# Decoding the last weight matrix during the attention and parking it in DRAM as float32

## The chip, the core and the metric

The kernel runs on one core of one Trainium2 chip. A core has five engines that run side by side, each with its own queue of instructions, which it takes strictly in order: PE (TensorE, matrix products; its weight loads are listed apart as PEld), DVE (VectorE), ACT (ScalarE), POOL (GpSimd) and SP (SyncE, which here only issues DMAs). Engines wait for one another through semaphores. Matrix products are accumulated in PSUM (eight banks), everything else lies in SBUF or in DRAM. The metric is the device time of one execution in microseconds (us); lower is better.

## What is computed

Three stages, each fed by the one before:

```python
attn_out = _attn_ref(q, k, v, f)                # 4 batches, 8 heads, 576 positions, 64 per head
x = attn_out.transpose(0, 2, 1, 3).reshape(2304, 512)
h = (x @ w1) * (x @ w2)                         # 512 -> 1024
x = (h @ w3) @ w_out                            # 1024 -> 1024 -> 512
h = x @ w_in                                    # 512 -> 2048
P = a[0] + a[1]*h + a[2]*h**2 + a[3]*h**3
Q = 1 + abs(b[0])*abs(h) + abs(b[1])*h**2
out = (P / (Q + 1e-6)) @ w_out2                 # 2048 -> 512
```

The attention adds to the scores a decay from the running sum of log f, masks the future, takes a softmax, and multiplies by v. All weight matrices arrive as float64. The kernel reads a weight as a pair of 32-bit integers and builds a float32 from the bits. That is called decoding here. Products that need more than one pass run three matmuls on a value split in two parts (high and low, with names that end in h and l).

## The kernel before

The program is one hand-ordered stream; the order in which Python issues an instruction is the order in its engine's queue.

**The decoder** (class Decoder, lines 38 to 114) has a list of jobs, one for each piece of a weight matrix: 128 rows by 256 columns (512 for w1 and w2). A ring of d_r buffers takes the loads of int64 pairs, and a second ring, d_f, the float32 result. One call of `step` works on four pieces at once, one in each phase: for piece k two DVE instructions (lines 99 and 102) and one of ACT (line 105, in place in d_r); for piece k-1 the POOL add (line 95) that finishes the float32; for piece k-2 the ACT copy that rounds the high part (line 91); for piece k-3 the subtraction that gives the low part (line 88, DVE or POOL in turn). Then `prefetch` issues the next load on SP (line 67), which waits until the ring's buffer is free, that is, for the POOL add of that same step. A list of n pieces needs n + 3 steps.

**The attention** (lines 547 to 651) runs 32 heads of five columns each; t counts the columns, n is the head, c the column. In each, PE makes scores, transposes the probabilities of an earlier column and multiplies by v; DVE takes the maximum (line 324), splits (line 381), evacuates ps_v (lines 256 and 411); ACT takes the exponential; POOL normalises (line 350). From head 9 on, `fill` puts matmuls of stage one (`gen_ab`, x times w1 and w2) between them, at 123 credits a matmul. Each pair of products is finished by an ACT copy a_sb (line 475) and a DVE product c_sb (line 478), which is stored to c_dr on SP. These free the PSUM banks for the next pair. `side_step` advances the decoder of w1 and w2, in the columns of DEC_AT and in every even column from t = 46, until it is done; the rest of it is run in head 13 at column 0 (line 416).

**The drain** (lines 699 to 711) comes next: the last batch of `gen_ab`, alone on PE, with four banks; after each 1250 credits `flush(2)` issues the copies and products that are due and the decoder makes one step. This second decoder, dec_, has a ring of four and takes w3 (32 pieces), w_out (16) and w_in (32), and in the kernel before also w_out2, called wo2 below (32).

**The w3 stage** (lines 738 to 763) multiplies w3 by w_out, so that stage three needs one product only; it transposes w3 row by row on PE and makes four decoder steps per row.

**Stage three** (lines 797 to 820) makes z = c times that product in nine blocks of four outputs, 24 matmuls an output, with banks in rotation. The block of c is loaded to cl and split (line 429, DVE, after an ACT copy to ch) one block ahead; z goes through z_sb (three buffers) to z_dr. The decoder makes one step after an even output and two after an odd one. The last stage (lines 891 to 921) uses w_in and wo2.

Of the kernel before, what the change touches and what calls it, by code (L numbers as in the profile page):

```python
# [10 lines left out]
F32 = mybir.dt.float32  # L11
# [8 lines left out]
P = 128  # L20
# [13 lines left out]
def raw(ap):  # L34
    return ap.bitcast(F32)


class Decoder:
# [8 lines left out]

    def __init__(self, nc, pool, name, size, n_ring, n_f32, jobs, lo_on="v", ahead=None):  # L50
        self.nc, self.jobs, self.lo_on = nc, jobs, lo_on
        self.ring = [pool.tile([P, size, 2], I32, name=f"{name}_r{i}") for i in range(n_ring)]
        self.f32 = [pool.tile([P, size], F32, name=f"{name}_f{i}") for i in range(n_f32)]
        self.at = 0
        self.sent = 0
        self.more = False
        self.ahead = n_ring if ahead is None else ahead
        self.prefetch()
# [18 lines left out]
    def step(self):  # L77

        nc, k, n = self.nc, self.at, len(self.jobs)
        if k >= n + (0 if self.more else 3):  # L80
            return False
        if 0 <= k - 3 < n:
            _, _, hi, lo = self.jobs[k - 3]
            if hi is not None:
                on = self.lo_on[(k - 3) % len(self.lo_on)]
                eng = nc.vector if on == "v" else nc.gpsimd
                v = self.like(self.place(k - 3), hi)
                eng.tensor_tensor(out=lo, in0=v, in1=raw(hi), op=ALU.subtract)
        if 0 <= k - 2 < n and self.jobs[k - 2][2] is not None:
            hi = self.jobs[k - 2][2]  # L90
            nc.scalar.copy(hi, self.like(self.place(k - 2), hi))
        if 0 <= k - 1 < n:
            u = self.place(k - 1).bitcast(I32)
            r = self.ring[(k - 1) % len(self.ring)]
            nc.gpsimd.tensor_tensor(out=u, in0=u, in1=r[:, :, 0], op=ALU.add)  # L95
        if k < n:
            r = self.ring[k % len(self.ring)]
            u, high, low = self.place(k).bitcast(I32), r[:, :, 1], r[:, :, 0]
            nc.vector.tensor_scalar(  # L99
                u, high, 3, -0x40000000, op0=ALU.logical_shift_left, op1=ALU.bitwise_or  # L100
            )
            nc.vector.scalar_tensor_tensor(  # L102
                out=u, in0=high, scalar=0x3FFFFFFF, in1=u, op0=ALU.bitwise_or, op1=ALU.bitwise_and
            )
            nc.scalar.activation(low, low.bitcast(U32), AF.Copy, scale=2.0**-29)  # L105
        self.at += 1
        self.prefetch()
        return True
# [9 lines left out]
def kernel(  # L118
# [40 lines left out]
    def pool(name, side, **kw):  # L159
        return tc.tile_pool(name=name, bufs=1, side=side, reuse_waits="tile", **kw)  # L160

    dram = ctx.enter_context(tc.tile_pool(name="dram", bufs=1, space=DRAM))
    crow_dr = dram.tile([NH, 2, S], F32, name="crow_dr")
    c_dr = dram.tile([P, NF1, NT], F32, name="c_dr")
    z_dr = dram.tile([P, NKC, NT], F32, name="z_dr")

# [264 lines left out]
    def gen_w12():  # L431
# [18 lines left out]
        xh.append(x1p.tile([P, NKC, S], F32R, name="xh1"))  # L450
        xl.append(x1p.tile([P, NKC, S], F32R, name="xl1"))

    def gen_ab(b, more=()):
        banks = [*ps_f, *more]
        X, L = xh[b % 2], xl[b % 2]
        n = 0
        FG = PIECE2 // P
        for g, hf, fi in itertools.product(range(NF1 // FG), range(2), range(FG)):
            ts_ = slice(HB * hf, HB * (hf + 1))
            fi += FG * g  # L460
            fs = slice(P * fi, P * (fi + 1))
            w12["dec"].run(4 * g + 3)
            outs = [t[:, 0:HB] for t in banks[n % (len(banks) // 2) * 2 :][:2]]
            for wi, nm in enumerate(("w1", "w2")):
                wh, wl = w12[nm]
                flush(len(banks) // 2)
                for kc in range(NKC):
                    mm(outs[wi], wh[:, kc, fs], X[:, kc, ts_], kc == 0, False)
                    yield 123
                    mm(outs[wi], wh[:, kc, fs], L[:, kc, ts_], False, False)  # L470
                    yield 123
                    mm(outs[wi], wl[:, kc, fs], X[:, kc, ts_], False, kc == NKC - 1)
                    yield 123
                if wi == 0:
                    pend.append(lambda a=a_sb[n % 2], o=outs[0]: nc.scalar.copy(a, o))

            def finish(c=c_sb[n % 3], a=a_sb[n % 2], fi=fi, hf=hf, o=outs[1]):
                nc.vector.tensor_tensor(out=c, in0=o, in1=a, op=ALU.mult)
                nc.sync.dma_start(c_dr[:, fi, S * b + HB * hf : S * b + HB * (hf + 1)], c)

            pend.append(finish)
            n += 1
# [6 lines left out]
    def flush(keep=0):  # L489
        while len(pend) > keep:  # L490
            pend.pop(0)()
# [5 lines left out]
    def fill(ns):  # L497
        credit[0] += ns
        while credit[0] > 0 and fillers:
            cost = next(fillers[0], "end")  # L500
            if cost == "end":
                fillers.pop(0)
            elif cost is None:
                break
            else:
                credit[0] -= cost
        if not fillers:
            credit[0] = 0.0
# [38 lines left out]
    for t in range(NCH * (NH + 1) + 2):  # L547
# [35 lines left out]
        flush()  # L583
        if t == 10:
            w12["dec"].ahead = 4
        if t in DEC_AT or (t >= 46 and t % 2 == 0):
            side_step()
        if t == 0:
            first_q(1)
# [61 lines left out]
                load_pair(p + 1, vf[(p + 1) % 2] if 2 * (p + 1) < N32 else v_raw, v)  # L651
    fill(1.0e9)
    flush()
    late.close()
    att.close()
    fillers.append(gen_ab(B - 1, (ps_v[:, 0:512], ps_v[:, 512:1024])))
# [48 lines left out]
    credit[0] = 0.0  # L705
    fill(3000.0)
    while fillers:
        fill(1250.0)
        flush(2)
        dec_.step()  # L710
    flush()
# [54 lines left out]
    wl_ = ctx.enter_context(pool("wl", "right"))  # L766
    woh = wl_.tile([P, NF2, DM], F32R, name="wo2h")
    wol = wl_.tile([P, NF2, DM], F32R, name="wo2l")
    for j in range(NF2):
        w_jobs(w_out2, j, woh, wol)  # L770
    dec_.more = False
    dec_.prefetch()
    ps1.close()
    psp = ctx.enter_context(tc.tile_pool(name="psp2", bufs=1, space=PSUM, reuse_waits="tile"))
    bank = [psp.tile([P, 512], F32, name=f"bank{i}") for i in range(8)]
# [21 lines left out]
    for i in range(NBLK):  # L797
        if 0 < i < NBLK - 1:
            load_c(i + 1)
        for e in range(NKC):  # L800
            g = NKC * i + e
            po = bank[g % 8][:, 0:T1]
            es = slice(P * e, P * (e + 1))
            for fi in range(NF1):
                mm(po, w3oh[:, fi, es], ch[i % 2][:, fi], fi == 0, False)
                mm(po, w3oh[:, fi, es], cl[i % 2][:, fi], False, False)
                mm(po, w3ol[:, fi, es], ch[i % 2][:, fi], False, fi == NF1 - 1)
            if g > 1:
                z_store(g - 2)
            if g > 0:  # L810
                z_out(g - 1)
            for _ in range(1 + g % 2):
                dec_.step()
            if i + 1 < NBLK:
                for x in ((), (0,), (2, 4), (6,))[e]:
                    split_c(i + 1, x)
        if i == NBLK - 2:
            load_z(0)
            for e in range(NKC):
                split_z(0, e)  # L820
# [137 lines left out]
```

## Time and profile before

| | us |
|---|---|
| median of three runs | 1047.26 (1044.64 to 1049.3) |
| the profiled execution | 1044.14 |
| its span, first to last instruction | 1042.3 |
| busy in the span: PE, DVE, ACT, POOL | 988.6, 811.1, 677.5, 386.2 |

The profile is one execution taken by the hardware profiler, with times from the start of the span. Busy times are sums over a stretch. Matmuls are pipelined, so a PE that is busy all the time may still be slowed. A row of waits tells which instruction stood idle for which. The granted clock is 1.00 at 2.4 GHz and 0.50 at 1.2 GHz.

### The profile page before, as it was taken

Reading aid. Unit: us, or ns where it says so; the run is one execution under the profiler, and the core shown is the slowest. Engines: PE = TensorE matmul, PEld = TensorE weight load, DVE = VectorE, ACT = ScalarE, POOL = GpSimd, SP = SyncE. Lnnn points to the kernel's source line nnn. Section 1 sums busy time; section 2 is a strip of 40 time slices with the busy share of each in tenths; the row PEclk is TensorE's granted clock in tenths of the full one; section 3 lists DMA queues with packets and bytes.
Section 4 is the critical chain, followed back from the end, with each engine's and each line's share of the span. In section 5 each row is a group of like instructions: output and inputs, shape, how many; then the busy total and the mean of one; then the engine's idle time right before and its main releaser. Section 6 shows DMA issues by size and latency. Waiting matters only on the chain.

```text
span 1042.3 us, 18664 instructions
## 1 busy us (share of the span) xinstructions
PE 988.6 (95%) x6224; PEld 898.4 (86%) x6224; DVE 811.1 (78%) x1809; ACT 677.5 (65%) x1558; POOL 386.2 (37%) x482
## 2 busy tenths in 40 slices
PE   6887889999999999899989899999999999999998
PEld 4666779999999999888789898988999889988897
DVE  5788886666666664989988886888888888888886
ACT  5566566666666663535655556777777777777775
POOL 7444564333333332544555551222222222222221
PEclk9999899999999999999999999999999999999999
DMA  5868454454544312676567771010010000000000
GB/s 132 213 155 183 129 149 105 110 131 111 125 113 124 98 41 85 205 219 190 174 192 243 244 245 58 1 31 31 1 31 31 31 31 1 31 31 1 31 1 31
DMA packets 119569, 106.59 MB, mean 102 GB/s; under 512 B 64816, under 2 KB 89904, under 8 KB 119472
## 3 DMA queue, kind: packets, MB, share of 16 engines
q1 hardware_dynamic: 119472, 105.40, 36.1%
q8 instruction: 49, 0.80, 0.3%
q14 instruction: 48, 0.39, 0.1%
HBM read 66.41 MB, written 19.02 MB: 82 GB/s over the span
## 4 chain that ended last, share of the span: by engine, by line
PE 73%; DVE 13%; DMA 6%; issue 4%; POOL 2%; ACT 2%; SPq 0%; POOLq 0%; DVEq 0%; ACTq 0%
PE bank L157 42%; PE ps_f L157 14%; PE ps_s L157 5%; PE ps_v L157 4%; PE ps_x L355 4%; DVE d_f L99 3%; DMA d_r<-in_moe_w_dram 2%; DMA d_r<-in_moe_w_out_dram 2%; DVE d_f L102 2%; PE ps_w L157 2%; DVE cl L429 1%; PE ps_v L246 1%; DMA z_dr<-z_sb 1%; DVE w3r L102 1%; DVE pr L324 1%
## 5 line engine op out<-in xcount | busy, mean ns | idle before, releaser
L855 POOL TENSOR_TENSOR gl<-pp,gh 128x384 fp32r<-128x384 f32 x96 | 98.0, 1021 | 314.5 <-ACT gh L854 251.4
L350 POOL TENSOR_SCALAR pr<-pr,st 128x128 f32<-128x128 f32 (+4 forms) x160 | 93.5, 595 | 194.0 <-DVE st L345 75.6
L324 DVE CUSTOM_DVE_ANT_0 pr<-ps_s,mask 128x128 f32<-128x128 f32 (+4 forms) x160 | 83.1, 523 | 72.3 <-PE ps_s L157 69.8
L157 PE MATMUL bank<-ch,wih 128*128 128x384 f32 x384 | 129.1, 336 | 2.0 <-DVE pp L876 2.0
L157 PE MATMUL bank<-ch,wil 128*128 128x384 f32 x384 | 129.4, 337 | 0.0
L157 PE MATMUL bank<-cl,wih 128*128 128x384 f32 x384 | 128.6, 335 | 0.0
L335 ACT ACTIVATE pr<-pr,st 128x128 f32<-128x128 f32 (+4 forms) x160 | 97.1, 607 | 32.1 <-DVE st L324 31.7
L95 POOL TENSOR_TENSOR d_f<-d_f,d_r 128x256 int32<-128x256 int32 (+1 forms) x96 | 88.1, 918 | 78.9 <-DVE d_f L102 36.4
L157 PE MATMUL bank<-wo2h,gl 128*128 128x512 f32 x288 | 113.9, 395 | 0.0
L157 PE MATMUL bank<-wo2l,gh 128*128 128x512 f32 x288 | 113.5, 394 | 0.0
L157 PE MATMUL bank<-wo2h,gh 128*128 128x512 f32 x288 | 113.5, 394 | 0.0
L862 ACT ACTIVATE h<-bank 128x384 f32<-128x384 f32 x96 | 47.0, 489 | 87.1 <-PE bank L157 86.5
L157 PE MATMUL bank<-cl,w3oh 128*128 128x256 f32 x288 | 82.1, 285 | 8.4 <-DVE cl L429 8.4
L379 ACT CAST pth<-ps_x 128x256 fp32r<-128x256 f32 (+1 forms) x96 | 44.5, 464 | 67.8 <-PE ps_x L355 51.3
L157 PE MATMUL ps_s<-kh,qs 128*128 128x128 f32 (+2 forms) x192 | 75.9, 395 | 8.6 <-DVE st L324 5.4
L157 PE MATMUL bank<-ch,w3ol 128*128 128x256 f32 x288 | 81.4, 283 | 1.4 <-DVE w3ol L755 1.4
L355 PE MATMUL ps_x<-ident,pr 128*128 128x128 f32 (+1 forms) x480 | 75.0, 265 | 6.8 <-POOL pr L350 3.3
L157 PE MATMUL bank<-ch,w3oh 128*128 128x256 f32 x288 | 81.2, 282 | 0.0
L105 ACT ACTIVATE d_r<-d_r 128x256 int32<-128x256 uint32 (+1 forms) x128 | 60.0, 471 | 31.4 <-DMA d_r<-in_moe_w_dram 23.9
L157 PEld LDWEIGHTS bank<-ch,wih 128*128 128x128 f32 x384 | 72.0, 188 | 6.9 <-DVE pp L876 2.7
L879 DVE SCALAR_TENSOR_TENSOR qv<-qv,rr 128x384 f32<-128x384 f32 x96 | 53.5, 558 | 31.3 <-ACT rr L874 31.3
L869 DVE SCALAR_TENSOR_TENSOR qv<-h,pb_abs,qv 128x384 f32<-128x384 f32 x96 | 59.1, 616 | 23.5 <-ACT qv L863 23.5
(167 smaller groups left out, 3076.3 us busy)
## 6 DMA issues: line engine op xcount, KB each, us to landing
d_r<-in_moe_w_out_dram SPq DMA_DIRECT2D x48, 256.0 KB
c_dr<-c_sb SPq DMA_DIRECT2D x64, 144.0 KB
cl<-c_dr SPq DMA_DIRECT2D x36, 256.0 KB
d_r<-in_moe_w_dram SPq DMA_DIRECT2D x16, 512.0 KB
d_r<-in_moe_w_dram SPq DMA_DIRECT2D x32, 256.0 KB
d_r<-in_moe_w_in_dram SPq DMA_DIRECT2D x32, 256.0 KB
kh<-kh SPq DMA_DIRECT2D x45, 144.0 KB
z_dr<-z_sb SPq DMA_DIRECT2D x36, 128.0 KB
```

The source lines that it names most:

```text
L95: nc.gpsimd.tensor_tensor(out=u, in0=u, in1=r[:, :, 0], op=ALU.add)
L105: nc.scalar.activation(low, low.bitcast(U32), AF.Copy, scale=2.0**-29)
L157: nc.tensor.matmul(o, lhsT, rhs, start=start, stop=stop)
L324: nc.vector.tensor_tensor_reduce(out=pr[0:r, OFF[c] + a : OFF[c] + b], in0=ps_s[(t + part) % 2][0:r, 0 : b - a], in1=mask[0:r, 512 - Q0[c] ...
L335: nc.scalar.activation(x, x, AF.Exp, bias=st[0:r, 0, c : c + 1], scale=-1.0, accum_out=st[0:r, 1, c : c + 1],)
L350: nc.gpsimd.tensor_scalar(x, x, st[0:r, 1, c : c + 1], 1.0, op0=ALU.mult, op1=ALU.mult)
L355: nc.tensor.transpose(ps_x[x][:, r * j : r * (j + 1)], pr[0:r, o + P * j : o + P * (j + 1)], ident[0:r, 0:r],)
L379: nc.scalar.copy(hi, src)
L855: nc.gpsimd.tensor_tensor(out=at(gl, j), in0=at(pp, j), in1=raw(at(gh, j)), op=ALU.subtract)
L862: nc.scalar.activation(at(h2, i), h, AF.Square)
L869: nc.vector.scalar_tensor_tensor(out=at(qv, i), in0=at(h2, i), scalar=pb_abs[:, 1:2], in1=at(qv, i), op0=ALU.mult, op1=ALU.add,)
L879: nc.vector.scalar_tensor_tensor(out=at(qv, i), in0=at(qv, i), scalar=QC, in1=at(rr, i), op0=ALU.add, op1=ALU.mult)
```

## The change

The 32 pieces of wo2 leave the list of dec_. A generator, `gen_wo2`, decodes them during the attention: it starts in head 13 at column 0, with one step at once, and then steps in columns 1 and 3 of every head until it is through. It has rings of three. It keeps float32 only and stores each piece to a new DRAM tensor, wo2_dr, one step after its POOL add. In stage three the matrix comes back by eight loads of 512 KB, one every four outputs, and is split there by one ACT copy and one subtraction of 512 columns after every second output. Stage three makes one decoder step an output. The drain gives 1600 credits a step.

```diff
@@ Decoder.step
+        if 0 <= k - 2 < n and len(self.jobs[k - 2]) > 4:
+            nc.sync.dma_start(self.jobs[k - 2][4], self.place(k - 2))
@@ new generator
+    def gen_wo2():
+        jobs = []
+        for j in range(NF2):
+            for g in range(0, DM, PIECE2):
+                cs = slice(g, g + PIECE2)
+                jobs.append((w_out2[P * j : P * (j + 1), cs], None, None, None, wo2_dr[j, :, cs]))
+        with pool("d3", "right") as rp:
+            dec_ = Decoder(nc, rp, "d3", PIECE2, 3, 3, jobs)
+            while dec_.step():
+                yield
@@ attention loop
-        if t in DEC_AT or (t >= 46 and t % 2 == 0):
+        if t == 65:
+            while side:
+                side_step()
+            side.append(gen_wo2())
+            side_step()
+        if t in DEC_AT or (46 <= t < 65 and t % 2 == 0) or (t > 65 and c in (1, 3)):
             side_step()
@@ drain
-        fill(1250.0)
+        fill(1600.0)
@@ before stage three
-    for j in range(NF2):
-        w_jobs(w_out2, j, woh, wol)
+    def load_wo2(j):
+        nc.sync.dma_start(raw(wol[:, j : j + 2]), wo2_dr[j : j + 2].rearrange("j p d -> p j d"))
+
+    def split_wo2(j):
+        nc.scalar.copy(woh[:, j], raw(wol[:, j]))
+        eng = nc.gpsimd if j % 3 == 2 else nc.vector
+        eng.tensor_tensor(out=wol[:, j], in0=raw(wol[:, j]), in1=raw(woh[:, j]), op=ALU.subtract)
+
+    load_wo2(0)
@@ stage three, after output g
-            for _ in range(1 + g % 2):
-                dec_.step()
+            dec_.step()
+            if g % 2 == 0 and 2 <= g < 34:
+                split_wo2(g // 2 - 1)
+            if g % 4 == 0 and 0 < g < 4 * (NF2 // 2):
+                load_wo2(g // 2)
```

ACT's queue at the start of head 13, before. The casts to pth and the copy xtmp serve the attention, w2h belongs to the decoder of w1 and w2:

```order
L379 CAST pth<-ps_x_85 128x2x128
L410 COPY xtmp<-ps_v 64x576
L91 CAST w2h<-d_f_171 128x2x256
L419 CAST xh_1705<-xr_135 128x576
L335 ACTIVATE pr,st<-pr,st 128x128
L475 COPY a_sb_102<-ps_f_1070 128x288
```

The same place after the change (line numbers are those of the changed kernel):

```order
L92 CAST w2h<-d_f_172 128x2x256
L108 ACTIVATE d_r_1707<-d_r_1707 128x256
L383 CAST pth<-ps_x_86 128x2x128
L414 COPY xtmp<-ps_v 64x576
L423 CAST xh_1702<-xr_136 128x576
L339 ACTIVATE pr,st<-pr,st 128x128
L490 COPY a_sb_103<-ps_f_1071 128x288
```

The first decode of wo2, which reads the buffer d_r that its load fills, now stands ahead of pth, xtmp and a_sb; w2h has moved up as well.

SP's queue in an even head, before (stores of c, small rows and stacked copies of q and k for the next pair of heads):

```order
L273 DMA kc_126<-crow_dr 2x576
L274 DMA qb_118<-crow_dr 2x576
L479 DMA c_dr<-c_sb_104 128x288
L300 DMA qb_117<-qs_113 64x576
L300 DMA qb_118<-qs_113 64x576
```

And after:

```order
L277 DMA kc_124<-crow_dr 2x576
L278 DMA qb_116<-crow_dr 2x576
L94 DMA wo_dr<-d_f_1711 128x256
L68 DMA d_r_1709<-in_moe_w_out_dram 128x512
L277 DMA kc_125<-crow_dr 2x576
L278 DMA qb_117<-crow_dr 2x576
L494 DMA c_dr<-c_sb_104 128x288
L304 DMA qb_116<-qs_112 64x576
L304 DMA qb_117<-qs_112 64x576
L94 DMA wo_dr<-d_f_1712 128x256
L68 DMA d_r_1707<-in_moe_w_out_dram 128x512
L304 DMA qs_112<-qs_113 64x576
```

A store of a finished piece (wo_dr is wo2_dr) and the load of a later one now stand twice a head between the copies of the next pair.

ACT's queue over some outputs of stage three, before (each z_sb is one output, each d_r one decoder step, ch the split of c):

```order
L778 COPY z_sb_5253<-bank_5768 128x256
L91 CAST wo2h<-d_f_4571 128x256
L105 ACTIVATE d_r_4569<-d_r_4569 128x256
L778 COPY z_sb_5251<-bank_5769 128x256
L91 CAST wo2h<-d_f_4572 128x256
L105 ACTIVATE d_r_4566<-d_r_4566 128x256
L91 CAST wo2h<-d_f_4573 128x256
L105 ACTIVATE d_r_4567<-d_r_4567 128x256
L428 CAST ch_5249<-cl_5250 128x512
```

And after:

```order
L807 COPY z_sb_5416<-bank_5918 128x256
L92 CAST wih<-d_f_4774 128x256
L108 ACTIVATE d_r_4772<-d_r_4772 128x256
L797 CAST wo2h<-wo2l 128x512
L432 CAST ch_5412<-cl_5413 128x512 x2
L807 COPY z_sb_5414<-bank_5919 128x256
L92 CAST wih<-d_f_4775 128x256
L108 ACTIVATE d_r_4769<-d_r_4769 128x256
L432 CAST ch_5412<-cl_5413 128x512
```

One decoder step an output is left, its pieces are w_in, and a cast that reads the loaded wo2l stands ahead of the split of c.

## Rows read from the trace of the kernel before

**Rows 1.** The chain of waits that ended last, shares by engine.

```profile
PE 73%; DVE 13%; DMA 6%; issue 4%; POOL 2%; ACT 2%; SPq 0%; POOLq 0%; DVEq 0%; ACTq 0%
```

**Rows 2.** Busy us (and instructions) by stretch: length, PE, PEld, DVE, ACT, POOL, clock, DMA share, GB/s.

```profile
186.00:400.00 214.00, 214.00 (x1592) 202.88 (x1590) 135.17 (x462) 132.08 (x343) 73.66 (x103) 1.00 0.40 102
404.00:466.00 62.00, 56.71 (x407) 55.30 (x407) 50.10 (x100) 26.81 (x71) 32.25 (x41) 0.97 0.63 195
466.00:518.00 52.00, 51.17 (x254) 41.94 (x253) 48.35 (x90) 28.11 (x68) 23.60 (x32) 1.00 0.59 187
518.00:632.00 114.00, 104.18 (x863) 102.23 (x862) 96.29 (x172) 65.05 (x173) 57.49 (x67) 0.97 0.70 221
613.00:631.00 18.00, 18.00 (x159) 17.88 (x159) 12.01 (x23) 9.35 (x25) 6.19 (x8) 1.00 0.60 190
```

**Rows 3.** PE's waits, 404 to 466 us: us in total, times, longest.

```profile
PE ps_v L157 <- DVE c_sb L478: 5.3, 6, 2.2
```

**Rows 4.** PE's longest wait from 518 to 632 us.

```profile
PE bank L157 <- DVE cl L429: 8.4, 7, 2.2
```

**Rows 5.** Busy times by stretch, one of three stretches at half clock.

```profile
549.40:552.70 3.30, 3.30 (x18) 3.30 (x17) 3.23 (x7) 2.24 (x6) 2.24 (x3) 0.50 0.90 268
```

**Rows 6.** Line 105 (one a step), 404 to 466 us: ns min/median/max, first and last start.

```profile
L105 ACT ACTIVATE d_r<-d_r x36: 431/443/452, 411.7 to 464.9; 128x256 int32<-128x256 uint32 x36
```

**Rows 7.** The drain's first loads on SP and ACT's first step, in order of time.

```profile
407.50 2.25 SPq L67 DMA_DIRECT2D d_r<-in_moe_w_dram  x4
...
411.69 0.44 ACT L105 ACTIVATE d_r<-d_r 128x256 int32<-128x256 uint32 x1 [5.60 <-DMA d_r<-in_moe_w_dram]
```

**Rows 8.** DVE, 518 to 632 us: groups (busy us, mean ns), then lines 99, 102 (min/median/max).

```profile
L99 DVE TENSOR_SCALAR d_f<-d_r 128x256 int32<-128x256 int32 x49 | 31.9, 652 | 7.9 <-DMA d_r<-in_moe_w_out_dram 6.0 <-DMA d_r<-in_moe_w_in_dram 1.9
L102 DVE SCALAR_TENSOR_TENSOR d_f<-d_r,d_f 128x256 int32<-128x256 int32 x49 | 27.2, 554 | 1.7
L429 DVE TENSOR_TENSOR cl<-cl,ch 128x512 fp32r<-128x512 f32 x33 | 26.8, 830 | 2.0 <-ACT ch L428 1.7 <-DMA z_dr<-z_sb 0.3
L88 DVE TENSOR_TENSOR wo2l<-d_f,wo2h 128x256 fp32r<-128x256 f32 x21 | 8.8, 418 | 0.0
...
L99 DVE TENSOR_SCALAR d_f<-d_r x49: 278/831/857, 518.0 to 621.3; 128x256 int32<-128x256 int32 x49
L102 DVE SCALAR_TENSOR_TENSOR d_f<-d_r,d_f x49: 424/426/853, 518.9 to 621.6; 128x256 int32<-128x256 int32 x49
```

**Rows 9.** DVE in head 20, the k split, in order of time.

```profile
255.41 0.76 DVE L256 SCALAR_TENSOR_TENSOR klt<-ps_v,kh 128x576 fp32r<-128x576 f32 x1 [1.37 <-ACT kh L254]
```

**Rows 10.** Head 13, columns 0 and 1, in order of time: ACT, SP, PE.

```profile
160.37 0.63 ACT L410 COPY xtmp<-ps_v 64x576 f32<-64x576 f32 x1
...
162.52 0.38 ACT L475 COPY a_sb<-ps_f 128x288 f32<-128x288 f32 x1
...
160.80 0.35 SPq L479 DMA_DIRECT2D c_dr<-c_sb  x1
...
163.26 0.29 PE L157 MATMUL ps_f<-xh,w1h 128*128 128x288 f32 x1
...
164.52 0.30 PE L355 MATMUL ps_x<-ident,pr 128*128 128x128 f32 x1 [0.83 <-DVE ptl L381]
```

**Rows 11.** PE's waits, 97 to 165 us, and the decoder's steps there.

```profile
PE ps_v L246 <- DVE xr L411: 4.3, 2, 2.8
PE ps_x L355 <- DVE st L345: 1.9, 3, 0.7
PE ps_x L355 <- DVE ptl L381: 1.6, 2, 0.8
...
L105 ACT ACTIVATE d_r<-d_r x9: 658/677/697, 99.0 to 148.7; 128x512 int32<-128x512 uint32 x9
```

**Rows 12.** A loaded stretch of stage three, and ACT's longest wait from 518 to 632 us.

```profile
575.00:584.00 9.00, 9.00 (x81) 9.00 (x81) 7.97 (x17) 6.56 (x18) 4.45 (x6) 1.00 0.91 290
...
ACT z_sb L778 <- DMA z_dr<-z_sb: 17.2, 7, 3.2
```

More of the change, by code (lines that the diff above doesn't have):

```diff
@@ L82, in step @@
         if 0 <= k - 3 < n:
-            _, _, hi, lo = self.jobs[k - 3]
+            hi, lo = self.jobs[k - 3][2:4]
             if hi is not None:
@@ L163 @@
     crow_dr = dram.tile([NH, 2, S], F32, name="crow_dr")
+    wo2_dr = dram.tile([NF2, P, DM], F32, name="wo2_dr")
     c_dr = dram.tile([P, NF1, NT], F32, name="c_dr")
@@ L653 @@
     flush()
+    while side:
+        side_step()
     late.close()
@@ L768 @@
     wol = wl_.tile([P, NF2, DM], F32R, name="wo2l")
-    for j in range(NF2):
-        w_jobs(w_out2, j, woh, wol)
     dec_.more = False
-    dec_.prefetch()
+    def load_wo2(j):
[5 more added lines that the diff above has]
+    load_wo2(0)
     ps1.close()
```

## The prediction

> **What bounds the kernel now.** I read the chain of waits first. It is PE for 73% and DVE for 13% [rows 1], so the question for every stage is whether PE ran all the time, and if not, who held it. The table of busy times by stage answers it [rows 2]. From 186 to 400 us (heads 15 to 31, the attention with stage-one matmuls as filler) PE is busy 214.00 of 214 us, while DVE is busy 63%, ACT 62% and POOL 34%: PE is the limit and the others have room. From 404 to 466 us (the drain: the last batch of stage one, with the decoder stepping in between) PE is busy 56.71 of 62. From 466 to 518 us (w3 times w_out) it is 51.17 of 52. From 518 to 632 us (stage three) 104.18 of 114, and DVE has 96.29 of those 114.
>
> PE's waits say who held it. In the drain it is DVE's product c_sb, 5.3 us in 6 times [rows 3]. In stage three it is the split of the c block, 8.4 us in 7 times [rows 4]. Both are short instructions that queue on DVE behind decoder steps. After the longer of these waits the granted clock stands at 0.50 for a stretch (1.2 GHz instead of 2.4). There are three such stretches of some 3.3 us, one in the drain and two in stage three; one of stage three is shown [rows 5]. A stretch at half speed gives half of it away, 1.65 us.
>
> So what can be won: in the drain 62 - 56.71 = 5.3 us of waiting and 1.65 us of clock, 7.0 us. In stage three 159 matmuls take 18 us where nothing holds PE, from 613 to 631 us [rows 2], 0.113 us each; the stage's 863 would take 97.7 us, they took 114, so 16.3 us are lost there. In the w3 stage 0.8 us. In the attention from head 15 on, nothing. The whole prize is 24 us.
>
> **The change, part by part.** The order of PE's instructions is the same before and after; only waits can move.
>
> *The drain.* With a credit of 1600 instead of 1250 per step, and 123 per matmul, a step follows every 13 matmuls and not every 10, and 28 decoder steps stand in the drain, not 36. A matmul of the drain is 56.71 / 407 = 0.139 us [rows 2], so PE now meets a step every 1.8 us, before every 1.4. The decoder's own pace there is 36 steps from 411.7 to 464.9 us, 1.5 us a step [rows 6]. Before, it was the slower of the two, fell behind, and c_sb with it; now it is the faster. Its late first load (issued 407.50, used at 411.69 [rows 7]) stays, and I leave 0.5 us for it: 6.5 us won, between 3 (if the late start alone makes half of the waits) and 7.
>
> *The w3 stage.* It runs 29 steps as before; only the pieces shift (8 more of w3, 8 fewer of w_in with its split). The transposes of a w3 row were 11 steps behind the decoder, now 3, some 4.5 us at 1.5. DVE is the tight engine, 48.35 of 52 us [rows 2]. I take 0, between +2 and -0.8.
>
> *Stage three.* 80 pieces and 3 steps of run-out make 83 steps; less 28 and 29, 26 are left for 36 outputs, where 54 stood. A step's two DVE instructions took 0.652 + 0.554 = 1.21 us here, 49 times [rows 8]; 23 stay, so 26 x 1.21 = 31 us leave DVE. The 21 old splits of wo2l took 8.8 us there; 11 new ones of twice the width, at the 0.83 us of the c split of the same shape [rows 8], take 9.1. A block of four outputs had 6 x 1.21 + 4 x 0.42 + 4 x 0.83 = 12.3 us of DVE, against 96 x 0.113 = 10.9 us of PE. It will have 4 x 1.21 + 2.7 x 0.42 + 5.3 x 0.83 = 10.4. That is why I expect PE to be the limit again, with little to spare until the 26 steps are through. Transfers per block stay at some 3.0 MB (1.0 of c, 0.5 of z, and 1.5 of int64 before, 1.0 of int64 and 0.5 of float32 now). Of 16.3 us I take 12, between 6 and 15.5, and leave 4 for the first block and for ACT waiting on the new loads.
>
> *The attention.* 32 pieces and 3 steps of run-out, two a head, heads 13 to 29. Each piece adds two DVE instructions, one of ACT, one of POOL, a load of 256 KB and a store of 128 KB on SP. The DVE pair costs 0.278 + 0.424 = 0.70 us at least and 1.71 at most [rows 8]; 32 pairs take 22 to 55 us of DVE's 79 free ones [rows 2]. What counts is where they stand. The pair of column 3 in an even head stands before the k split, which waits 1.37 us for its input anyway [rows 9]. The pair of column 1 stands a column ahead of the q split, the next thing there that frees ps_v for PE. SP is moved past too: each load waits for POOL's add, and the loads of q, k and the stacked rows of the next pair queue behind it; they are needed about a head later. I price all of this at 1 us, between 0 and the rival below.
>
> *The first step* has no cover. At the start of head 13 the generator asks for its first load and steps at once, so DVE and ACT stand still for that load. SP is free for it after the c store, 160.80 + 0.35 [rows 10]. The only row with a fresh ring shows 4.2 us from issue to use [rows 7]. ACT would then go on at 165.3 with xtmp, which it began at 160.37 before, and the copy a_sb, 2.5 us behind it, would end near 168 and not at 162.9; PE wants that bank at 163.26 [rows 10]. That is 4.7 us, less the 0.83 us that PE waits there already, 3.9. The row had four loads in flight, here it is one of three, so I take 3.5 us; a wait that is added can't give time back, so 0 and 5 are the ends. The Trainium skill (DMA: Bandwidth & Descriptors, Rules for kernel authors) has the rule that this step breaks: issue a DMA early, compute, and wait for it late. The same page (Latency and other measured facts) gives about 2 us as the fixed cost of a DMA; with 256 KB at the 290 GB/s of [rows 12] the load would take 2.9 us, an estimate, and the loss would be 2.6 instead of 3.5.
>
> *The sum.* -6.5 + 0 - 12 + 1 + 3.5 = -14. The profiled execution took 1044.14 us (span 1042.3), so it would take 1030. The three runs have their median 3 us higher, at 1047.26, so the forecast for a median is 1033. Best ends: -7 - 0.8 - 15.5 + 0 + 0 = -23, 1024. Worst ends without a rival: -3 + 2 - 6 + 3 + 5 = +1.
>
> **The rivals.** *The attention pays (slower).* In heads 9 to 13 the older decoder steps did hold PE: the longest waits there, all for DVE, come to 4.3 + 1.9 + 1.6 = 7.8 us for 9 steps on pieces of 512 [rows 11], 0.87 us a step. The new pieces are half as wide. At half the price 32 steps cost 14 us and the time is 1046, no change; at the full price 28 us, 1060, slower. It decides from (18.5 - 3.5) / 32 = 0.47 us a step. Against it: the longest of these waits is for the evacuation of ps_v, and the old steps stood in the column of that evacuation in even heads; the new ones do not. The Trainium skill (SBUF — State Buffer, Who interferes with whom) lets a DVE instruction with two SBUF inputs be blocked for the whole of a POOL instruction that reads SBUF. The second decode instruction has two, and its rows reach from 424 to 853 ns [rows 8], which agrees; it is the upper end that I used.
>
> *The load takes the place of the decode.* In stage three ACT's copy of wo2l stands two outputs (5.4 us) behind its load, and that load behind 1 MB of c. The queues moved 290 GB/s there at a share of 0.91 for 9 us on end, and ACT waited 17.2 us for z stores to land [rows 12]. 1.75 MB at that rate need 6 us, after some 2.5 us of issuing; ACT would stand still 3 us a block, and the c splits behind it come late by 1 to 1.5 us in 7 blocks: 8 of the 12 us are gone, 1041.
>
> *The drain keeps its time*, since the late first load and not the pace sets it: 6 us less won, 1039.
>
> **How the numbers follow.** Forecast (1024 to 1038): 0.62. Load in place of decode: 0.14. Drain unchanged: 0.10. Attention pays at half price 0.08, at full price 0.06. The range leaves out these last two and little else: 1023 to 1044. A measurement of this kernel can tell about 0.5% (5.2 us) from no change, so faster means below 1042. Faster: 0.62 + 0.10 + 0.10 of the load's 0.14 = 0.82; same 0.04 + 0.08 = 0.12; slower 0.06.
>
> **What would show it.** In the drain PE's wait for c_sb falls from 5.3 us to about 1, and no stretch at 0.50 remains. Stage three takes about 102 us instead of 114, with PE's wait for the c split under 3 us. In head 13 ACT and DVE wait for the load from w_out, and PE stands for some 3 us near 164 us; from head 15 on PE stays busy. If PE is busy less than 97% between 186 and 400 us, the attention paid. If ACT's largest wait in stage three is for the wo2l load, the second rival holds. If the drain still takes 60 us, the third.

## The result and the profile after

The changed kernel took 1029.09 us, the median of four runs (1027.81 to 1029.91), against 1047.26: a ratio of 0.9827, with a 95% interval of 0.9803 to 0.9851. The forecast was 1033 in a range of 1023 to 1044, faster with 0.82. Direction and size were right.

The page of the changed kernel: its span, busy time by engine, and the shares of the chain that ended last.

```profile
span 1026.0 us, 18623 instructions
...
PE 985.7 (96%) x6224; PEld 898.1 (88%) x6224; DVE 794.6 (77%) x1799; ACT 673.9 (66%) x1542; POOL 383.3 (37%) x476
...
PE 84%; DVE 4%; DMA 2%; issue 2%; ACT 2%; SPq 0%; POOL 0%; DVEq 0%; POOLq 0%; ACTq 0%
```

PE is busy 985.7 us, 988.6 before: the work on PE is the same, and its gaps shrank from 53.7 to 40.3 us. DVE's share of the chain fell from 13% [rows 1] to 4%.

Busy times by stretch of the changed kernel, stages as in [rows 2], and one stretch of head 13. The columns are those of [rows 2].

```profile
190.00:404.00 214.00, 214.00 (x1589) 202.57 (x1588) 149.68 (x513) 139.02 (x369) 93.14 (x131) 1.00 0.57 149
404.00:461.50 57.50, 57.50 (x434) 57.24 (x433) 44.59 (x86) 23.97 (x64) 26.80 (x34) 1.00 0.61 185
461.50:512.70 51.20, 50.84 (x254) 41.94 (x252) 45.48 (x85) 26.85 (x62) 20.86 (x28) 1.00 0.57 181
512.70:616.00 103.30, 101.86 (x866) 101.22 (x865) 71.82 (x118) 56.55 (x140) 39.90 (x40) 1.00 0.70 223
...
163.65:170.35 6.70, 5.49 (x22) 5.00 (x23) 6.36 (x17) 4.09 (x13) 3.69 (x5) 0.50 0.46 126
```

In the attention PE is still busy all the time; DVE took 14.5 us more there (149.68 against 135.17) and ACT 7, and nobody waited for it. The drain has no gap left. In stage three DVE fell from 96.29 to 71.82 us. What is new is the last row: 6.7 us at half clock in head 13, where the kernel before had none.

From stage to stage, by the first and last matmuls of each in the two traces:

| stage | before, us | after, us | difference | forecast |
|---|---|---|---|---|
| heads 0 to 12 (same code) | 159.8 | 157.8 | -2.0 | 0 |
| head 13 (the first step) | 12.73 | 17.90 | +5.2 | +3.5 |
| heads 14 to 30 | 210.18 | 210.55 | +0.4 | +1 |
| head 31 and drain | 84.18 | 76.07 | -8.1 | -6.5 |
| w3 stage | 51.32 | 50.60 | -0.7 | 0 |
| stage three | 114.24 | 103.19 | -11.05 | -12 |
| last stage | 409.9 | 409.95 | 0 | 0 |

The differences add up to -16.3, the spans differ by 1042.3 - 1026.0 = 16.3. The first line is no effect of the change: in the ten profiles of kernels that share the code of heads 0 to 8, those heads took 97.1 to 101.0 us, and the half-clock stretches fell elsewhere from one to the next. In the eight that share the code of heads 0 to 12 these took 157.8 to 163.1 us. So a single profile is uncertain by some 3 us there, and the experiments are read stage by stage.

PE's waits from 513 to 616 us (us in total, times, longest). From 404 to 462 us, and from 176 to 404 us, the same view has no row at all.

```profile
PE bank L160 <- DVE cl L433: 0.9, 2, 0.7
PE bank L160 <- DVE w3ol L777: 0.5, 1, 0.5
```

The 8.4 us of [rows 4] are 0.9, the 5.3 us of [rows 3] are gone.

Stage three on DVE, 512 to 616 us: groups of instructions, to be held against [rows 8].

```profile
L433 DVE TENSOR_TENSOR cl<-cl,ch 128x512 fp32r<-128x512 f32 (+1 forms) x37 | 27.8, 776 | 18.5 <-ACT ch L432 18.3
L102 DVE TENSOR_SCALAR d_f<-d_r 128x256 int32<-128x256 int32 x25 | 14.3, 572 | 0.0
...
L105 DVE SCALAR_TENSOR_TENSOR d_f<-d_r,d_f 128x256 int32<-128x256 int32 x26 | 12.3, 474 | 0.9
L799 DVE TENSOR_TENSOR wo2l<-wo2l,wo2h 128x512 fp32r<-128x512 f32 x11 | 8.2, 746 | 8.7 <-ACT wo2h L797 8.6
```

The 49 pairs of decode instructions have become 26, and each costs 0.572 + 0.474 = 1.05 us where it cost 1.21. Both windows take in the last pairs of the w3 stage: stage three itself has 23 pairs, as counted (26 steps less the 3 of run-out), and had 47. DVE now waits 18 us for ACT in front of the c split; those are waits of an engine that has time.

Head 13 in order of time: SP's load, ACT and DVE, PE; the brackets give the idle time before.

```profile
159.19 1.40 SPq L68 DMA_DIRECT2D d_r<-in_moe_w_out_dram  x3
...
162.08 0.29 DVE L102 TENSOR_SCALAR d_f<-d_r 128x256 int32<-128x256 int32 x1 [2.20 <-DMA d_r<-in_moe_w_out_dram]
162.08 0.44 ACT L108 ACTIVATE d_r<-d_r 128x256 int32<-128x256 uint32 x1 [5.18 <-DMA d_r<-in_moe_w_out_dram]
...
164.43 0.38 ACT L490 COPY a_sb<-ps_f 128x288 f32<-128x288 f32 x1
...
164.86 0.61 PE L160 MATMUL ps_f<-xh,w1h 128*128 128x288 f32 x1 [3.44 <-ACT a_sb L490]
```

This is the predicted chain link by link: the load, ACT standing behind it, the copy a_sb late, PE late. PE stood for 3.44 us, and the half-clock row above begins while it stood.

### The profile page after: what moved, and what is told of

Same layout as the page of the kernel before. It is cut to its first block, busy times and chain, and to the rows that moved or that the text cites. A ratio compares the mean times of both kernels' runs of the same rounds, so it can differ in the third digit from the quotient of the medians.

```text
span 1026.0 us, 18623 instructions
## 1 busy us (share of the span) xinstructions
PE 985.7 (96%) x6224; PEld 898.1 (88%) x6224; DVE 794.6 (77%) x1799; ACT 673.9 (66%) x1542; POOL 383.3 (37%) x476
## 4 chain that ended last, share of the span: by engine, by line
PE 84%; DVE 4%; DMA 2%; issue 2%; ACT 2%; SPq 0%; POOL 0%; DVEq 0%; POOLq 0%; ACTq 0%
PE bank L160 47%; PE ps_f L160 19%; PE ps_v L160 6%; PE ps_s L160 5%; PE ps_x L359 4%; PE ps_v L250 1%; PE ps_w L160 1%; DVE pr L328 1%; DVE d_f L102 1%; DMA d_r<-in_moe_w_in_dram 1%; PE ps_v L251 0%; DMA z_dr<-z_sb 0%; DMA d_r<-in_moe_w_dram 0%; DVE cl L433 0%; DMA d_r<-in_moe_w_out_dram 0%
## 5 line engine op out<-in xcount | busy, mean ns | idle before, releaser
L339 ACT ACTIVATE pr<-pr,st 128x128 f32<-128x128 f32 (+4 forms) x160 | 97.1, 607 | 32.2 <-DVE st L328 31.8
L911 DVE SCALAR_TENSOR_TENSOR qv<-qv,rr 128x384 f32<-128x384 f32 x96 | 53.7, 559 | 31.3 <-ACT rr L906 31.3
```

What stands on the lines that cost most here:

```text
L339: nc.scalar.activation(x, x, AF.Exp, bias=st[0:r, 0, c : c + 1], scale=-1.0, accum_out=st[0:r, 1, c : c + 1],)
L911: nc.vector.scalar_tensor_tensor(out=at(qv, i), in0=at(qv, i), scalar=QC, in1=at(rr, i), op0=ALU.add, op1=ALU.mult)
```

## The experiments

Each theory is told in the expectation. All runs are set against the kernel before, whose median was 1047.6 to 1047.8 us in these sessions.

### The first step of head 13, one pause later

```diff
             dec_ = Decoder(nc, rp, "d3", PIECE2, 3, 3, jobs)
+            yield
             while dec_.step():
```

The decoder asks for its loads at column 0 and takes its first step at column 1.

> The changed kernel with one more yield between the first three loads and the first decode step of wo2, so that the step comes one column later. Theory (in head 13 ACT and DVE stand for the load, 5.2 us, and PE then stands 3.4 us and runs at half clock): ACT's wait for the load from w_out in head 13 is gone or under 0.5 us, PE has no wait over 1 us there, heads 13 to 31 take about 5 us less than in the changed kernel, and the time is 1024 us. Rival (what head 13 loses is the three loads and the store on SP, or the added DVE work): the wait stays above 2 us somewhere else in heads 13 and 14 and the time stays at 1028 to 1029 us.

Measured: 1026.35 us (1025.83 to 1026.55), ratio 0.9798 (0.9778 to 0.9818). Head 13 took 13.23 us, against 17.90. The same place in order of time, and PE's only wait from 158 to 240 us:

```profile
163.46 1.40 SPq L68 DMA_DIRECT2D d_r<-in_moe_w_out_dram  x3
...
164.26 0.38 ACT L491 COPY a_sb<-ps_f 128x288 f32<-128x288 f32 x1
166.99 0.44 ACT L108 ACTIVATE d_r<-d_r 128x256 int32<-128x256 uint32 x1 [2.35 <-DMA d_r<-in_moe_w_out_dram]
```

```profile
PE ps_f L160 <- DVE c_sb L494: 1.1, 1, 1.1
```

ACT still waits, 2.35 us, where the theory had under 0.5, but a_sb stands ahead of the wait now, PE stands 1.1 us, and no half-clock stretch follows. So the loss of head 13 came from what was queued behind the wait, not from the wait itself. The time fell by 2.7 us only, where 5 were expected: in this profile heads 0 to 12, whose code is the same, took 162.0 us against 157.8.

### The drain at its old credit

```diff
-        fill(1600.0)
+        fill(1250.0)
```

> The changed kernel with 1250 credits a step in the drain again (36 steps there, not 28); everything else as changed. Theory (the drain waited because PE met a step every 1.4 us and the decoder makes one in 1.5 us): PE's wait for c_sb is back at 4 to 6 us, a stretch at clock 0.50 may come back, the drain is 6 to 8 us longer, stage three up to 2 us shorter for its 8 fewer steps, time 1033 to 1036 us. Rival (the drain is shorter because wo2's loads and pieces are gone from the list): drain as in the changed kernel, time 1027 to 1029 us.

Measured: 1041.19 us (1035.33 to 1042.61), ratio 0.993 (0.9903 to 0.9957). Head 31 and the drain took 84.51 us, 8.4 more, and PE's wait from 404 to 476 us is that of [rows 3]:

```profile
PE ps_v L160 <- DVE c_sb L493: 6.7, 6, 2.2
```

The drain's gain comes from the credit alone. The span is 11.4 us longer; 3.6 of them lie in heads 0 to 13, whose code is the same, and stage three took 1.3 back. The time is some 5 us above the 1033 to 1036 expected, which this leaves in part unexplained.

### The kernel before with the new credit only

```diff
-        fill(1250.0)
+        fill(1600.0)
```

> The kernel before with 1600 credits a step in the drain alone; wo2 is still decoded in the list, so 8 more steps fall to the later stages. Theory: the drain gets 6 to 8 us shorter as in the changed kernel, and stage three and what follows it get 5 to 10 us longer, since 58 steps are left for 54 places and DVE has no room there: time 1044 to 1050 us, no gain. Rival (the drain's pace is a gain of its own): stage three keeps its 114 us and the time is 1039 to 1041 us.

Measured: 1049.32 us, ratio 1.0023 (1.0007 to 1.0038). The drain gained its 8.3 us, stage three lost 3.5 and the last stage 8.2. PE's wait for the c split, and the first 16 us of the last stage (columns as in [rows 2]):

```profile
PE bank L157 <- DVE cl L429: 14.1, 9, 2.2
```

```profile
629.00:645.00 16.00, 7.06 (x33) 6.74 (x32) 14.07 (x25) 10.41 (x25) 7.82 (x11) 0.69 0.45 132
```

The steps that the drain no longer makes are made at the end, where PE is busy 7 us of 16 and the clock is low. So the larger credit needs the other part of the change: it is worth 8 us because 32 pieces have left the list. The move needs the credit less: without it, in the run before this one, the time was still 6 us below that of the kernel before.

### The steps of the attention in columns 0 and 2

```diff
-        if t in DEC_AT or (46 <= t < 65 and t % 2 == 0) or (t > 65 and c in (1, 3)):
+        if t in DEC_AT or (46 <= t < 65 and t % 2 == 0) or (t > 65 and c in (0, 2)):
```

> The changed kernel with the steps in columns 0 and 2 of each head in place of 1 and 3; same work. Theory (what matters is the place: in column 0 of an even head the pair stands ahead of the evacuation of ps_v, line 415, as the older steps of w1 and w2 do): PE's wait for line 415 appears in even heads 14 to 28, 0.5 to 1.5 us each, and the attention is 4 to 12 us longer, time 1033 to 1041 us. Rival (the attention has room enough anywhere, the older steps cost because they are twice as wide): no wait over 1 us in total, time 1028 to 1030 us.

Measured: 1035.28 us, ratio 0.9878 (0.985 to 0.9907). Heads 14 to 30 took 215.59 us, 5.0 more. PE's waits from 176 to 404 us, where the changed kernel has none:

```profile
PE ps_v L250 <- DVE xr L415: 2.4, 8, 0.4
PE ps_x L359 <- DVE ptl L385: 0.5, 2, 0.2
```

The same steps two places on cost 5.0 us, 0.16 us a step, with PE waiting for the evacuation that the prediction named. The listed waits are 2.9 of the 5.0; from the start of one matmul to the start of the next, the same ten places lose 4.4. No stretch at half clock lies in these heads.

### Stage three at its old rate of steps

```diff
-            dec_.step()
+            for _ in range(1 + g % 2):
+                dec_.step()
```

> The changed kernel, but stage three takes its decode steps at the old rate, two at every odd output, so the last stage's weights (wi) are decoded one and a half steps an output and are through after some 17 outputs in place of 26. The work in the stage is the same. Theory (the rate within a block is what made PE wait for cl before, not the stage's total): VectorE would need about 3.1 us of c splits, six steps of 1.80 us and 1.0 us of wo2 splits for a block of four outputs, 14.9 us against the block's 10.9, as long as steps are left, so PE waits for cl again at about four blocks, 1 to 1.5 us each, and stage three becomes 4 to 6 us longer than 103.2; time 1034 (1031 to 1037). Rival (VectorE's total over the stage decides, 99 us before and 72 after, and the order within it is absorbed): stage three within 1 us of 103.2, time 1029.

Measured: 1041.04 us, ratio 0.9925 (0.9904 to 0.9946). Stage three took 113.24 us, 10.05 more. PE's waits from 509 to 630 us:

```profile
PE bank L160 <- DVE cl L433: 7.3, 8, 2.2
PE bank L160 <- ACT ch L432: 1.7, 2, 1.2
```

The rate within a block decides, not the sum over the stage, since the sum is that of the changed kernel and nearly the whole gain is lost. The theory has the mechanism and half the size: the waits are 9.0 us in place of the 4 to 6, and a stretch of 6.8 us at half clock at 561 us, in which PE was busy 5.3 us and which it did not count, gives some 2.6 more. (Against that, 2.83 us an output in the changed kernel are 2.72 here, see the end.)

### Five steps a head in the attention

```diff
-        if t in DEC_AT or (46 <= t < 65 and t % 2 == 0) or (t > 65 and c in (1, 3)):
+        if t in DEC_AT or (46 <= t < 65 and t % 2 == 0) or t > 65:
```

> The changed kernel with a step of the fourth matrix in every column from head 13 on, five a head, so that it is decoded within about eight heads in place of eighteen. Theory (the attention takes a step for nothing only at columns 1 and 3, since at 0 and 2 it stands ahead of the evacuations that PE waits for; the run with columns 0 and 2 paid 0.28 us a head): heads 13 to 20 grow by 0.3 to 1 us each, heads 14 to 31 together by 2 to 8 us, with PE waits for xr (L415) and ptl (L385) in heads 14 to 21 and none after; time 1032 to 1037. Rival (VectorE had 30 per cent idle, a third of it is taken, nothing waits): heads 14 to 31 within 0.5 us of 210.5, time 1029. Third (VectorE is overrun there, the steps being 1.5 to 2 us each beside a busy GpSimd): plus 15 us or more.

Measured: 1050.93 us, ratio 1.0038 (1.0019 to 1.0056), 0.4% slower than the kernel before. Heads 14 to 30 took 230.86 us, 20.3 more, all of it before head 20, when the pieces are through. That is the third forecast in size, though not by its reason. PE's longest waits from 176 to 404 us, and busy times over heads 14 to 19 (columns as in [rows 2]):

```profile
PE ps_x L359 <- DVE ptl L385: 4.1, 4, 2.4
PE ps_f L160 <- DVE c_sb L493: 2.8, 2, 2.5
PE ps_v L250 <- DVE qs L260: 2.2, 1, 2.2
```

```profile
178.00:273.00 95.00, 82.67 (x553) 75.48 (x553) 70.58 (x217) 55.17 (x147) 47.92 (x65) 0.93 0.74 203
```

All of PE's waits there come to 12.4 us. The clock of 0.93 is four stretches of 3.4 us at 0.50, one each in heads 15, 17, 18 and 19, which lost 4 to 6 us each; heads 14 and 16, with as many steps and no such stretch, lost 0.5 to 0.6. PE was busy 13.3 us of the four stretches, so they gave away 6.7. Waits and clock together are 19.1 of the 20.3 us.

DVE, for which PE waited, was held up in the decoder. Its two instructions from 176 to 275 us, and then line 102 in the changed kernel, from 190 to 404 us:

```profile
L105 DVE SCALAR_TENSOR_TENSOR d_f<-d_r,d_f 128x256 int32<-128x256 int32 x28 | 17.2, 614 | 1.0
L102 DVE TENSOR_SCALAR d_f<-d_r 128x256 int32<-128x256 int32 x28 | 10.6, 377 | 15.2 <-DMA wo_dr<-d_f 5.7 <-issue 5.0 <-POOL pr L354 4.4
```

```profile
L102 DVE TENSOR_SCALAR d_f<-d_r 128x256 int32<-128x256 int32 x27 | 7.7, 285 | 0.0
```

DVE was not overrun: it stood still for 15.2 us in front of line 102, 5.7 of them for a buffer of the ring of three whose store had not landed. And the two instructions took longer than in the changed kernel.

The longest of them stand beside POOL. One line 105 on DVE, POOL's work in the same microseconds, and then line 105's shortest, median and longest time here (28 steps) and in the changed kernel (29 steps):

```profile
190.71 1.67 DVE L105 SCALAR_TENSOR_TENSOR d_f<-d_r,d_f 128x256 int32<-128x256 int32 x1
...
190.50 1.60 POOL L244 TENSOR_TENSOR vhl<-v_raw,vhl 128x640 fp32r<-128x640 f32 x1
...
L105 DVE SCALAR_TENSOR_TENSOR d_f<-d_r,d_f x28: 424/426/1667, 177.1 to 264.1; 128x256 int32<-128x256 int32 x28
```

```profile
L105 DVE SCALAR_TENSOR_TENSOR d_f<-d_r,d_f x29: 424/425/427, 178.6 to 352.5; 128x256 int32<-128x256 int32 x29
```

The step of 190.71 us took 1.67 us in place of 0.42: it ended 0.28 us after POOL's instruction, which had begun 0.21 us before it. All 13 of the 28 that took more than 0.43 us ran beside a POOL instruction that had begun before them, the other 15 beside none. In the changed kernel no line 105 of the attention overlapped a POOL instruction by more than 0.1 us.

So the attention takes two steps a head for almost nothing and not five. 20.3 us for the 30 steps of heads 14 to 19 are 0.68 us a step: this is the rival "the attention pays", past its turning point of 0.47.

### The old steps of heads 9 to 12 in columns 1 and 3

This one stands on the first experiment's kernel.

```diff
-        if t in DEC_AT or (46 <= t < 65 and t % 2 == 0) or (t > 65 and c in (1, 3)):
+        if t in DEC_AT or (46 <= t < 65 and (c in (1, 3) or t in (49, 59))) or (t > 65 and c in (1, 3)):
```

> The kernel with one more pause before the first step (the one that took head 13 back to 13.2 us), and in it the ten steps of w1 and w2 in heads 9 to 12 put at columns 1 and 3 and twice at column 4, where they stood at columns 0, 2, 4 and 1, 3 by turns. Their number and the heads they fall in stay. Theory (place decides: these steps ahead of column 0's evacuations cause PE's waits for L415, 4.3 us, and L425, 1.6 us, in that stretch): heads 9 to 12 go from 63.4 to about 59, time 1022 (1020 to 1025). Rival (VectorE is 84 per cent busy there, 63 of 79 us, and its sum sets the length wherever the steps stand): heads 9 to 12 within 1 us of 62 to 63, time 1026.

Measured: 1021.72 us (1019.91 to 1025.02), ratio 0.9757 (0.9732 to 0.9782). Heads 9 to 12 took 58.9 us, 4.5 less. PE's longest waits from 97 to 162 us, first of the first experiment's kernel:

```profile
PE ps_v L250 <- DVE xr L415: 4.3, 2, 2.7
PE ps_x L359 <- DVE st L349: 1.9, 3, 0.7
PE ps_f L160 <- DVE xl L425: 1.6, 1, 1.6
```

then of this one:

```profile
PE ps_v L160 <- DVE ptl L385: 4.1, 2, 2.5
PE ps_x L359 <- DVE st L349: 1.8, 3, 0.7
PE ps_f L160 <- DVE xl L425: 1.6, 1, 1.6
```

The size came out, the reason only in part. The wait for line 415 went as expected, but one for line 385 came in its place and line 425's stayed; all waits there fell from 10.5 to 8.9 us. Most of the 4.5 us is clock: 10.2 us at half clock in that stretch before, 3.4 here, which is some 3.2 us of PE's time. That part may be accident, since the changed kernel, with the same code there as the first experiment's, had 6.8 us at half clock. A fairer price of the place alone is 1.7 us: with 6.8 us at half clock each, the four heads took 60.6 us in the changed kernel and 58.9 in the last experiment below, which has this edit.

### Four of these steps earlier

On the kernel just shown; DEC_AT holds the columns with a step in heads 0 to 8.

```diff
-    DEC_AT = {4, 10, 16, 22, 28, 34, 40}
+    DEC_AT = {4, 8, 13, 18, 23, 26, 28, 33, 36, 38, 43}
...
-        if t in DEC_AT or (46 <= t < 65 and (c in (1, 3) or t in (49, 59))) or (t > 65 and c in (1, 3)):
+        if t in DEC_AT or t in (48, 51, 53, 56, 58, 61) or (t > 65 and c in (1, 3)):
```

> The last kernel (one more pause in head 13, w1 and w2's steps at columns 1 and 3), with four of the ten steps of heads 9 to 12 moved into heads 1 to 8, which then have eleven in place of seven, six staying behind. It tells place from sum for heads 9 to 12, since the last run shortened them by 4.5 us but only 1.6 us of that was PE's waits, 3.4 us being half clock. Theory (VectorE's sum: 57 of 65 us busy there, so four steps of about 3.5 us less shorten it; heads 0 to 8 have VectorE busy 64 of 86 us and take them in part): heads 9 to 12 go from 58.9 to 51 to 55, heads 0 to 8 from 97.3 to 98 to 103, time 1018 (1014 to 1022). Rival (place alone, the sum not felt): heads 9 to 12 within 1.5 us of 58.9 and heads 0 to 8 longer by what the steps cost, time 1023 or more.

Measured: 1021.17 us (1018.58 to 1022.71), ratio 0.9751 (0.9712 to 0.979), no better. Heads 9 to 12 fell to 50.8 us, heads 0 to 8 rose to 105.1. Busy times by stretch (heads 1 to 8, then 9 to 12), first of the kernel it is built on, then of this one:

```profile
11.00:97.30 86.30, 74.11 (x523) 56.22 (x524) 63.96 (x190) 54.84 (x149) 42.25 (x68) 1.00 0.75 173
97.30:156.20 58.90, 50.08 (x351) 45.86 (x350) 51.99 (x130) 39.44 (x99) 37.53 (x39) 0.97 0.59 155
```

```profile
11.00:105.00 94.00, 79.78 (x522) 60.83 (x523) 71.56 (x200) 59.71 (x157) 53.81 (x73) 0.93 0.73 180
105.00:156.00 51.00, 48.27 (x353) 44.58 (x352) 41.63 (x121) 35.58 (x91) 27.77 (x34) 1.00 0.57 142
```

In heads 9 to 12 less DVE work made the stretch shorter, as the theory has it: 10.4 us of DVE less, 7.9 us shorter, of which 1.7 are a half-clock stretch that is gone. Heads 1 to 8, where DVE had 22 us free, paid it back: 7.6 us more DVE and 7.7 us longer. Most of that is clock: these heads have three stretches at 0.50, 13.7 us in all, and the kernel it is built on has none there, so that PE was busy 5.7 us more for the same matmuls. In the ten other profiles heads 0 to 8 had 0 to 6.8 us at half clock. That the added DVE work brought the low clock about is not shown.

### The splits of wo2 after the decode

Also on the kernel of columns 1 and 3.

```diff
-            if g % 2 == 0 and 2 <= g < 34:
-                split_wo2(g // 2 - 1)
+            if g >= 20:
+                split_wo2(g - 20)
```

> The last kernel with the sixteen splits of the fourth matrix put at outputs 20 to 35 of stage three, one an output, in place of every second output from 2 on; the loads stay. Theory (stage three's remaining waits for cl, 1.3 us, come from blocks in which VectorE has c splits, wi's decode steps and these splits together, 11.3 us against 10.9): the waits at outputs 8 to 20 fall under 0.4 us, none is new behind them since the decode is through, stage three 101 to 102 against 102.6; time 1020.5, hardly to be told from 1021.7. Rival (the late splits crowd the z splits and the last c splits, and the last stage waits for wo2): stage three plus 2 us or the last stage later by 1 to 3 us, time 1024.

Measured: 1018.26 us (1017.52 to 1018.65), ratio 0.9724 (0.9695 to 0.9753), the best kernel here, 1% below the changed one. Stage three took 99.35 us, 3.3 less. PE's waits from 490 to 620 us:

```profile
PE bank L160 <- DVE pp L909: 2.0, 2, 1.3
...
PE bank L160 <- DVE cl L433: 0.2, 1, 0.2
```

The wait for the c split is 0.2 us in place of 1.3, and none is new; the one for pp lies in the last stage and is there in the other kernels too. That is what the theory expected, but the run does not show its cause: ACT's waits for the loads of wo2, 4.1 us in the kernel it is built on, are gone as well, and in the changed kernel one of them held the c split too (next section). The gain is larger than the 0.6 to 1.6 us expected for the stage, since PE also ran at its better pace throughout (below); in the kernel it is built on, outputs 21 to 35 took 2.83 us each and not 2.72.

## Why the prediction held, point by point

**The drain: forecast -6.5, measured -8.1.** The mechanism is confirmed from both sides, by the old credit in the new kernel (+8.4) and the new credit in the old kernel (-8.3). The term was low because it left 0.5 us for the late first load, which cost PE nothing to be seen, and because 7.0 us was taken for all that there was to win. The busy time of 56.71 us that it started from was itself stretched: it held 407 matmuls, 0.139 us each, and now 434 take 57.50 us, 0.132 each. At that pace the 407 need 53.9 of the 62 us, and 8.1 could be won. The rival "the drain keeps its time" fell.

**The w3 stage: 0, measured -0.7**, inside its ends.

**Stage three: -12, measured -11.05.** The count of 23 pairs that stay is exact; 24 left and not 26, since the 49 of [rows 8] took in two of the w3 stage. A step at 1.05 us and a split at 0.75 were cheaper than the 1.21 and 0.83 used, and PE's wait went from 8.4 to 0.9 us. That the rate within a block matters, and not the stage's total, is shown by the run at the old rate; that it is DVE's time which had to come under the block's 10.9 us is worked out and not shown by itself. The 4 us left over were put down to the first block and to ACT waiting for the new loads, and that is half of what was lost. Outputs at 2.72 us make 36 x 2.72 = 97.9 us; 5.3 us are lost. The first output took 1.4 us over, output 8 took 1.0 over, and the 27 outputs from 9 to 35 ran 0.11 us slower each with no wait at all, 3.0 us, which no term foresaw. ACT did wait for the loads of wo2, as the second rival says, but little. ACT's waits, 513 to 616 us:

```profile
ACT z_sb L807 <- DMA z_dr<-z_sb: 6.1, 3, 3.0
ACT wo2h L797 <- DMA wo2l<-wo_dr: 4.1, 5, 1.5
```

The second row is 4.1 us in five waits, where the rival needed 3 us in each of seven blocks. The wait for z stores fell from 17.2 us [rows 12] to 6.1. The rival fell in its size, but not altogether: PE's one wait after the first output, at output 8, stands behind such a load. ACT and PE there, in order of time:

```profile
533.15 0.62 ACT L797 CAST wo2h<-wo2l 128x512 fp32r<-128x512 f32 x1 [1.15 <-DMA wo2l<-wo_dr]
...
539.07 0.38 PE L160 MATMUL bank<-cl,w3oh 128*128 128x256 f32 x1 [0.68 <-DVE cl L433]
```

The casts of c to ch stand behind that cast on ACT, DVE stood 2.37 us for them, and the split that PE wanted came 0.68 us late. Without the 1.15 us it would have come in time; that is an estimate from these rows and was not run alone.

**The attention from head 14 on: +1, measured +0.4.** The DVE pair cost 0.285 + 0.425 = 0.71 us, the lower end of 0.70 to 1.71. The upper end rested on POOL standing in the way, and in columns 1 and 3 it does not: every line 105 took 424 to 427 ns. With five steps a head it does, up to 1667 ns. The Trainium skill (SBUF — State Buffer, Who interferes with whom) says that whichever engine issues first holds the shared ports for its whole instruction, for a DVE instruction with two SBUF inputs, if POOL's reads SBUF, and for a `tensor_scalar` in its two-port mode alike. The rows agree on both: line 105 in the run with five steps, and line 99 of the kernel before, with its one input, from 278 to over 800 ns [rows 8]: each of those over 800 began while an add of POOL ran. In which mode line 99 ran no row tells. The rival that the attention pays fell for this change, but the argument against it was the right one, the place: columns 0 and 2 cost 5.0 us, and all five columns, which also raise the rate, made the kernel slower than before.

**The first step: +3.5, measured +5.2.** Here a part of the term failed. The wait was right: PE stood 3.44 us, 0.83 of which it had before [rows 10], so 2.6 us were added. That is less than 3.5, because the load was used 2.9 us after its issue and not 4.2. That agrees with the 2.9 us which the prediction estimated from the Trainium skill (DMA: Bandwidth & Descriptors, Latency and other measured facts). In the first experiment the same load was used 3.5 us after its issue, between that and the row with four. What was left out is that PE's clock was 0.50 for 6.7 us from within the wait on; PE was busy 5.49 us of them, so 2.7 us were given away. 2.6 and 2.7 make 5.3, and 5.2 were measured. The prediction had counted this loss for the waits that it removed, and not for the one that it added. One pause took back 4.7 us of head 13.

**The sum: -14, measured -16.3 between the two profiles, -18.2 between the medians.** The drain, the attention and the w3 stage came out 1.6, 0.6 and 0.7 us better than their terms, stage three and head 13 1.0 and 1.7 worse. That these nearly cancel is luck, and the 2.0 us of heads 0 to 12 are accidental. The step from the profile to a median was taken at +3 us, since the median of before stood 3 us over its profiled execution; after, the profiled execution took 1027.81 us, only 1.3 below the median.

## What to carry to other kernels

Move work from a stage whose tight engine sets its pace to one where another engine does, but count it by the block, not by the stage: two steps a head cost 0.4 us, five cost 20 us, and the same steps in stage three at one and a half per output lost what one per output had won. Put the first step of a generator, which waits for its load, behind what other engines need next, since everything behind it on the queue waits too. A wait on PE can cost more than its own length: in head 13, 2.6 us of added wait came with 2.7 us lost to the half clock. When a change takes work out of a stage, look for the second thing it makes possible: the larger credit gained nothing alone (1049.32 us), the move without it took 1041.19, and both together 1029.09.

## What the runs showed of the hardware

PE has two paces at full clock. In stage three matmuls of 256 columns with no wait between them ran either 0.113 us or 0.118 us apart, 2.72 or 2.83 us for an output of 24. Busy times over the same 60 us, first of the changed kernel, then of the best one:

```profile
545.00:605.00 60.00, 60.00 (x511) 60.00 (x511) 40.24 (x64) 33.84 (x81) 21.64 (x22) 1.00 0.71 228
```

```profile
545.00:605.00 60.00, 60.00 (x532) 60.00 (x531) 36.40 (x60) 34.70 (x84) 16.81 (x19) 1.00 0.67 213
```

Both rows have PE busy all the time at a granted clock of 1.00, and 511 matmuls against 532. In every trace the pace changed only at an output with a wait (outputs are counted from 0): in the changed kernel at output 8, to 2.83 us from there on; in the kernel before to 2.83 at output 4 and back at output 8; with five steps a head at output 8 to 2.83 and at output 20 back to 2.72; with the old steps in columns 1 and 3 at output 20 to 2.83; in the first experiment's kernel there were waits at 8 and 20 and the pace stayed at 2.72. The best kernel had no wait worth the name and kept 2.72 throughout. What sets the pace when PE starts again was not found; so 3.0 us of the changed kernel's stage three are explained by a row but not by a cause.
